# Decode attention on one core: values seven heads behind the keys, another choice of groups whose value product streams V, and two heads' output rows multiplied earlier

## Chip, cores, metric

One core of one Trainium2 chip. The metric is the device time of one execution in microseconds (us); the profile's span is 1.7 to 1.9 us shorter, as it leaves out the ends (2.0 to 3.0 us in three runs of before_64). PE is the matmul engine, PEld its weight loads, DVE, ACT and POOL the vector, scalar and general engines, SP the engine that issues the loads.

## The reference

A decode step for one token. The part that fills the time is attention over 32 heads, each with 4096 keys and values of 128 elements in bf16: 1 MB of keys and 1 MB of values per head.

```python
q = (x @ wq).reshape(B, Sq, Hq, Dh)...            # 32 heads of 128
k = k_cache[:, :, Sk - W:, :]; v = v_cache[...]     # W = 4096
p = softmax(einsum("bhqd,bhkd->bhqk", q, k) * Dh**-0.5)
o = einsum("bhqk,bhkd->bhqd", p, v)
s = o.reshape(B, Sq, Hq * Dh) @ wo                  # wo: 4096 x 512
# ... x + s * g, where g comes from a small MLP
```

## The kernel before

The kernel is one software pipeline over the heads. In step `i` it loads and handles the keys of head `i`, and the values of head `h = i - LAG`. Even heads get their scores on DVE (`k_vector`), odd heads on PE (`k_turn`, `k_scores`). Four heads form a group that shares a softmax.

The value product (PV) has two forms. In the ordinary one V is the stationary operand and 32 matmuls of one column make `o`; in the "moved" one V streams through PE, in 8 matmuls of 512 columns:

```python
MOVED = (1, 4); LAG = 6; K_BUFS = 12; V_BUFS = 7
...
def v_head(h, v):
    if g in MOVED:
        for c in range(0, NC, 4):
            nc.tensor.matmul(s["ov"][32 * hl:32 * hl + 4], lhsT=s["pT"][:, hl, c:c + 4],
                             rhs=v[:, c:c + 4, :], ...)
    else:
        for c in range(NC):
            nc.tensor.matmul(s["oT"][:, hl:hl + 1], lhsT=v[:, c, :], rhs=s["pT"][:, hl, c:c + 1], ...)
```

The tail, where the change works (cuts are marked `...`):

```python
for i in range(H + LAG):
    h = i - LAG
    kn = load_kv(k_pool, A_k_cache, i) if i < H else None
    ...
    if h == H - 1:
        load_rows(h_part, H - G - h_part)      # wo rows of heads 26, 27
    v = load_kv(v_pool, A_v_cache, h) if h >= 0 else None
    ...
    if h == H - 1:
        load_rows(H - G, G - 1)                # heads 28 to 30
        load_rows(H - 1, 1)                    # head 31: the last load
    ...
    if i == H:
        v_head(h, v); sm_turn(LG); y_block(few_block - 1); sm_exp(LG); ox_spread(few_block)
    ...
    if h >= H - G:
        v_out(h, 1)                            # ACT: o of head h, divided by its sum

for h in range(h_part, H):                     # 6 heads, 24 matmuls
    y_head(h)                                  # o of head h times its rows of wo
```

## Time and profile before

| | before |
|---|---|
| time, median of the first 3 runs | 197.33 us (197.11 to 197.45) |
| span of the profiled run | 196.0 us |
| loads from HBM | 78.84 MB, 402 GB/s over the span |
| busy: PE, DVE, ACT | 71%, 64%, 43% |
| chain that ended last, by engine | DMA 69%, PE 21%, issue 4% |

The row of DMA in the page's slices tells that transfers fill the time from the start to the last two slices. The chain of waits tells what the very end hangs on. It is found from the end backwards and printed in order of time: each piece is what released the next one. Both are shown in the prediction.

### The profile page before, as it was taken

The numbers are of one execution on the slowest core, as the hardware profiler recorded it, in microseconds if no ns is written. First come the engines' busy times: TensorE is split into PE (matmuls) and PEld (weight loads), VectorE is DVE, ScalarE is ACT, GpSimd is POOL, SyncE is SP. The second block draws the span as 40 slices with busy tenths as digits, with TensorE's granted clock in tenths as the row PEclk, the third lists the DMA queues.
The fourth block names the chain that finished last, engine by engine and source line by source line (L and its number), as shares of the span: only waits on it lengthen the run. The fifth ranks groups of instructions, "written<-read, shape, count | busy, mean of one in ns | idle before, by whom it ended". The sixth has DMA issues, their size and how long they took to land.

```text
span 196.0 us, 4913 instructions
## 1 busy us (share of the span) xinstructions
PE 138.4 (71%) x2204; PEld 105.6 (54%) x2204; DVE 124.7 (64%) x124; ACT 84.5 (43%) x180; POOL 5.9 (3%) x13
## 2 busy tenths in 40 slices
PE   0559797672796899787785828399977757289752
PEld 0453435561795555486365817335547756178542
DVE  1520259998988949795969195495979391853001
ACT  2003028870757443946074707407282619064210
POOL 2110007000000000000000000000000000000000
PEclk9999859967555579995596555759997558558555
DMA  6999899999999999999999999999999999999970
GB/s 199 408 476 448 363 413 420 418 428 428 423 428 420 428 418 428 418 428 423 428 421 428 421 428 425 423 428 423 426 426 421 426 421 428 423 426 426 414 270 4
DMA packets 11516, 79.15 MB, mean 404 GB/s; under 512 B 1384, under 2 KB 2248, under 8 KB 2504
## 3 DMA queue, kind: packets, MB, share of 16 engines
q1 hardware_dynamic: 11344, 78.85, 96.3%
q8 instruction: 17, 0.28, 0.6%
q10 hardware_dynamic: 152, 0.00, 0.0%
q14 instruction: 3, 0.02, 0.0%
HBM read 78.84 MB, written 0.00 MB: 402 GB/s over the span
## 4 chain that ended last, share of the span: by engine, by line
DMA 69%; PE 21%; issue 4%; DVE 2%; ACT 1%; POOL 1%; SPq 0%; POOLq 0%
DMA kv<-in_A_v_cache_dram 37%; DMA kv<-in_A_k_cache_dram 30%; PE oT L389 3%; PE qb_ps L240 3%; PE ov L379 3%; PE pt L290 3%; DMA x_bf<-in_A_x_dram 2%; PE hr_ps L214 2%; PE y_ps L141 1%; PE a_ps L203 1%; PE hr_ps L211 1%; PE qT_ps L231 1%; PE sT L297 1%; PE den_ps L334 1%; ACT kt L291 1%
## 5 line engine op out<-in xcount | busy, mean ns | idle before, releaser
L291 ACT COPY kt<-pt 128x1024 bf16<-128x1024 bf16 x64 | 60.2, 1028 | 58.9 <-PE pt L290 58.9
L281 DVE TENSOR_REDUCE sS<-prod 128x32 f32<-128x4096 bf16 x16 | 70.7, 4420 | 0.6
L290 PE MATMUL pt<-ident_bf,kv 128*128 128x128 bf16 x512 | 46.0, 268 | 8.4 <-DMA kv<-in_A_k_cache_dram 6.9
L290 PEld LDWEIGHTS <-kv 128*128 128x128 bf16 x512 | 41.9, 124 | 13.2 <-DMA kv<-in_A_k_cache_dram 7.9
L278 DVE TENSOR_TENSOR prod<-kv,q_bc 128x4096 bf16<-128x4096 bf16 x16 | 36.6, 2288 | 14.1 <-DMA kv<-in_A_k_cache_dram 11.8
L389 PE MATMUL oT<-pT,kv 128*128 128x1 bf16 x768 | 23.8, 165 | 15.3 <-DMA kv<-in_A_v_cache_dram 10.8
L389 PEld LDWEIGHTS <-kv 128*128 128x128 bf16 x768 | 22.9, 103 | 17.2 <-DMA kv<-in_A_v_cache_dram 12.0
L379 PE MATMUL ov<-kv,pT 128*4 128x512 bf16 x64 | 18.5, 441 | 0.0
L297 PE MATMUL sT<-qT_bf,kt 128*128 128x1 bf16 x512 | 16.3, 164 | 2.5 <-ACT kt L291 2.3
L297 PEld LDWEIGHTS <-kt 128*128 128x128 bf16 x512 | 14.7, 99 | 4.8 <-ACT kt L291 3.0
L404 ACT ACTIVATE o<-oT,rden 128x1 bf16<-128x1 f32 x32 | 6.1, 263 | 13.9 <-PE oT L389 9.3
L336 DVE RECIPROCAL rden<-den_ps 128x4 f32<-128x4 f32 x8 | 1.5, 182 | 14.7 <-PE den_ps L334 14.7
L379 PEld LDWEIGHTS <-pT 128*4 128x4 bf16 x64 | 5.3, 92 | 10.2 <-issue 5.4
L311 PE MATMUL mt_ps<-ident_f,m 128*4 128x128 f32 x8 | 2.5, 315 | 6.4 <-DVE m L305 5.9
L321 PE MATMUL mb_ps<-md,ones_f 4*128 4x4 f32 x16 | 3.6, 292 | 4.4 <-DVE md L315 4.4
L313 DVE TENSOR_REDUCE mx<-mt_ps 4x1 f32<-4x128 f32 x8 | 2.2, 278 | 7.0 <-PE mt_ps L311 7.0
L321 PEld LDWEIGHTS mb_ps<-md,ones_f 4*128 4x128 f32 x16 | 2.9, 223 | 6.5 <-DVE md L315 6.5
L240 PE MATMUL qb_ps<-wq_sb,xn_rep 128*128 128x512 bf16 x16 | 6.3, 584 | 0.0
L217 DVE COPY hr<-hr_ps 1x512 f32<-1x512 f32 x1 | 0.7, 679 | 8.4 <-PE hr_ps L214 8.4
L443 PE MATMUL yr_ps<-wo,ox 128*1 128x512 bf16 x16 | 5.2, 483 | 0.0
L323 ACT COPY mb<-mb_ps 128x4 f32<-128x4 f32 x8 | 1.5, 185 | 8.6 <-PE mb_ps L321 8.6
L206 ACT ACTIVATE a_bf<-a_ps 128x10 bf16<-128x10 f32 x1 | 0.2, 179 | 11.5 <-PE a_ps L203 11.5
(110 smaller groups left out, 94.1 us busy)
## 6 DMA issues: line engine op xcount, KB each, us to landing
kv<-in_A_k_cache_dram SPq DMA_DIRECT2D x32, 1024.0 KB, 19.6
kv<-in_A_v_cache_dram SPq DMA_DIRECT2D x32, 1024.0 KB, 19.6
wq_sb<-in_A_wq_dram SPq DMA_DIRECT2D x1, 4096.0 KB, 18.1
wo<-in_A_wo_dram SPq DMA_DIRECT2D x3, 1024.0 KB, 20.3
w_sb<-in_B_w_dram SPq DMA_DIRECT2D x1, 1376.0 KB
w_sb<-in_B_w_dram SPq DMA_DIRECT2D x1, 1024.0 KB, 8.9
w_sb<-in_B_w_dram SPq DMA_DIRECT2D x1, 512.0 KB, 3.7
wo_rows<-in_A_wo_dram SPq DMA_DIRECT2D x1, 384.0 KB, 16.3
```

The lines of the kernel that those rows point to most:

```text
L214: nc.tensor.matmul(hr_ps[:], lhsT=a_bf[0:m, i:i + 1], rhs=w4_sb[0:m, i, :], start=False, stop=(i == len(chunks) - 1))
L240: nc.tensor.matmul(qb_ps[:], lhsT=xn_rep[:, c, :], rhs=wq_h[:, c, 2 * i:2 * i + 8:2, :], start=(c == 0), stop=(c == KC - 1))
L278: nc.vector.tensor_tensor(out=prod[:], in0=kn[:], in1=q_bc[:, h // 2:h // 2 + 1, :].to_broadcast([P, NC, Dh]), op=ALU.mult)
L281: nc.vector.tensor_reduce(out=st[g]["sS"][:, hl // 2, :], in_=prod[:], axis=AX.X, op=ALU.add)
L290: nc.tensor.transpose(pt[:, i, :], kn[:, b * 8 + i, :], ident_bf[:])
L291: nc.scalar.copy(out=kts[h][:, b * 8:(b + 1) * 8, :], in_=pt[:])
L297: nc.tensor.matmul(st[g]["sT"][:, hl // 2, c:c + 1], lhsT=kt[:, c, :], rhs=qT_bf[:, h:h + 1], start=True, stop=True)
L321: nc.tensor.matmul(mb_ps[:], lhsT=ones_f[0:G, :], rhs=s["md"][:], start=True, stop=True)
L379: nc.tensor.matmul(s["ov"][32 * hl:32 * hl + 4], lhsT=s["pT"][:, hl, c:c + 4], rhs=v[:, c:c + 4, :], start=False, stop=c == NC - 4, skip_g ...
L389: nc.tensor.matmul(s["oT"][:, hl:hl + 1], lhsT=v[:, c, :], rhs=s["pT"][:, hl, c:c + 1], start=(c == 0), stop=(c == NC - 1))
L404: nc.scalar.mul(o_blk[h // 8][:, (h + k) % 8:(h + k) % 8 + 1], st[g]["oT"][:, hl + k:hl + k + 1], st[g]["rden"][:, hl + k:hl + k + 1])
L443: nc.tensor.matmul(yr[i][:], lhsT=ox_blk[i][:, t:t + 1], rhs=wo_blk[i][:, t, :], start=(t == 0), stop=(t == 7))
```

## The change

The intent is to give PE one more step between a group's softmax and its value products, so that PE is not behind the loads at the end, and to take work out of the last stretch. The core of the diff:

```diff
-LAG = 6
+LAG = 7
-MOVED = (1, 4)
+MOVED = (2, 4)
...
-        if h == H - 1:
+        if h == H - 2:
             load_rows(h_part, H - G - h_part)
...
-            for g in done(i, LAG + 5):
+            for g in done(i, LAG + 4):        # ox_spread, ox_pick; y_wide moves likewise
...
-            for g in done(i, LAG + 1, LG):
+            for g in done(i, G + 3, LG):
                 sm_den(g)
...
         if h >= H - G:
             v_out(h, 1)
+        if h == H - 2:
+            for r in range(h_part, H - G):    # heads 26 and 27, right after PV30
+                y_head(r)
-    for h in range(h_part, H):
+    for h in range(H - G, H):
         y_head(h)
```

The rest of the diff sorts the last seven steps anew.

More of the change, by code (lines that the diff above doesn't have):

```diff
@@ L503 @@
                 sm_exp(g)
-            for g in done(i, LAG + 1, LG):
+            for g in done(i, G + 3, LG):
                 sm_den(g)
-            for g in done(i, LAG + 5):
+            for g in done(i, LAG + 4):
                 if g % 2 == 1:
@@ L509 @@
         if i == H:
-            v_head(h, v)
             sm_turn(LG)
@@ L514 @@
             sm_exp(LG)
-            ox_spread(few_block)
-        elif h >= 0:
-            if i == H + 1:
-                ox_pick(few_block)
-            if i == H + 2:
-                ox_few(few_block)
-                sm_den(LG)
-            v_head(h, v)
-            if i == H + 2:
-                y_block(few_block)
+        if i == H + 1:
+            ox_pick(few_block)
+        if i == H + 2:
+            ox_few(few_block)
+            sm_den(LG)
+        if h >= 0:
+            v_head(h, v)
+        if i == H:
+            v_out(H - 2 * G, 2)
+            ox_spread(few_block)
+        if i == H + 2:
+            y_block(few_block)
+            rows_add(y_ps, one_f, y_row, False)
+        if i == H + 3:
+            v_out(H - 2 * G + 2, 2)
         if i < H:
@@ L532 @@
                     v_out(G * g, G)
-            for g in done(i, LAG + 6):
+            for g in done(i, LAG + 5):
                 if g % 2 == 1:
@@ L536 @@
                     y_keep(g // 2)
-        if i == H - 1:
-            v_out(H - 2 * G, 2)
-        if i == H + 1:
-            v_out(H - 2 * G + 2, 2)
-            rows_add(y_ps, one_f, y_row, False)
         if h >= H - G:
             v_out(h, 1)
-    for h in range(h_part, H):
+        if h == H - 2:
+            for r in range(h_part, H - G):
+                y_head(r)
+    for h in range(H - G, H):
         y_head(h)
```

## The prediction

> **What bounds the kernel now.** I read the page first: the totals and the slices, then the DMA view, then the chain that ended last, and last the timeline of the final 25 us. The slices come first, because an average would hide what differs by stage.
>
> ```profile
> PE   0559797672796899787785828399977757289752
> PEclk9999859967555579995596555759997558558555
> DMA  6999899999999999999999999999999999999970
> GB/s 199 408 476 448 363 413 420 418 428 428 423 428 420 428 418 428 418 428 423 428 421 428 421 428 425 423 428 423 426 426 421 426 421 428 423 426 426 414 270 4
> ...
> q1 hardware_dynamic: 11344, 78.85, 96.3%
> q8 instruction: 17, 0.28, 0.6%
> ```
>
> The DMA row has a 9 in every slice from the sixth to the thirty-eighth, at some 425 GB/s. No engine has that: PE is at 71% of the span, DVE at 64%, ACT at 43%. So the kernel is a stream of 78.85 MB that must pass (78.85 MB at 425 GB/s is 185.5 us of the 196.0), a start before the stream is full, and a tail after the last bytes. The change loads the same tensors in the same pieces, so it cannot shorten the stream. It can only touch what the end waits for. That is in the chain:
>
> ```profile
> 180.74 0.83 PE oT L389 x32
> 181.57 0.53 PE y_ps L141 x6
> 182.10 1.04 issue
> 183.13 0.58 PE y_ps L141 x2
> ...
> 186.56 0.96 PE oT L389 x32
> ...
> 187.86 0.83 PE oT L389 x26
> 188.69 1.40 issue
> 190.10 0.31 PE oT L389 x6
> ...
> 190.43 0.27 ACT o L404
> ...
> 190.75 0.99 PE oT L389 x32
> 191.74 0.77 PE y_ps L141 x13
> ```
>
> The groups of 32 are the value products (PV) of heads 27, 29, 30 and 31 (28 is in between). Two things are to be seen. From 172 us on, the chain is on PE and no longer on a DMA, so PE is behind the stream. And two pauses called "issue" (1.04 and 1.40 us) break it in the middle of instructions that wait for no data. How far behind PE is follows from the landing times of the last loads:
>
> ```profile
> 172.27 0.34 SPq L77 DMA_DIRECT2D kv<-in_A_v_cache_dram  x1
> DMA to landing us min/median/max: 17.7/17.7/17.7
> ...
> 177.06 2.32 SPq L77 DMA_DIRECT2D wo_rows<-in_A_wo_dram  x1
> ```
>
> The first two lines are the load of V31, the values of the last head: it lands at 172.27 + 17.7 = 189.97 us, and its product starts at 190.75, so PE is 0.78 us late. The third is the last load of all, the output rows of head 31. By the DMA view of its own window it takes 14.2 us to landing: 177.06 + 14.2 = 191.26 us. The last four matmuls, which need those rows, end at 191.74 + 0.77 = 192.51 us. So PE's lateness is worth little: about 1 us lies between the last landing and the end of PE.
>
> **What the skill says.** "DMA: Bandwidth & Descriptors", section "Where 436 GB/s comes from", puts the ceiling of 16 engines at 435 GB/s. The trace agrees with 425 to 428 in the plateau: there is nothing left in it. "Runtime: NRT & Kernel Launch", section "Instruction fetch mechanics", says that an engine's instructions come by DMA in blocks of 16 KiB, that is 256 instructions, mostly hidden. The trace has 17 packets with 0.28 MB on the instruction queue, 16 KB each, and I take the two pauses for fetches that were not hidden, as PE runs a dense stretch there: from the first pause to the second it runs about 256 instructions. "TensorE: Matmul & The Clock Gate", Part 1, says that the array runs at half or full clock by its recent activity. The trace agrees: 32 PV matmuls take 0.78 us where the granted clock was 0.93 (176 to 180 us) and 0.99 us at 0.50 in the tail. I expect the tail at 0.50 after the change too.
>
> **The change part by part.**
>
> Values seven heads behind the keys. K7 goes into the queue ahead of V0, and every later key is one load ahead of where it was against the values. A 1 MB load takes 2.45 us (the keys and values are issued at that distance: 62.17, 64.68, 67.11). K31 landed at 172.21 with seven values still to come, and should land at about 169.8 with eight to come. K30, for DVE, moves by more than that, since the third block of output weights now stands between K30 and K31. The softmax of the last group and the scores of head 31, which made PE late, thus move about 2.45 us earlier, while V31 stays at 189.97. That more than covers the lateness of 0.78 us. At the start the queue holds one more load when V0 has to wait for the end of the weights' use (V0 is issued at 30.52; the queue waited 9.0 us for the query product). The queue did not run dry there before (413 and 420 GB/s in the slices around it), so nothing is gained.
>
> Rows of heads 26 and 27 at PV30. They are 8 matmuls out of the 24 that ran after PV31. Rows of 24 took 192.51 - 191.74 = 0.77 us after PV31, so 8 of them are worth at most 0.77 x 8/24 = 0.26 us. But the rows of head 31 also wait for ACT's o of head 31, about 0.3 us after PV31 ends (0.27 us and two waits of 0.02 to 0.04), during which the first rows run for nothing. Of the 0.26 about 0.2 should be seen. Their load moves ahead of V30 and delays V30 by some 0.6 us (256 KB), to 187.5, which is not what the end waits for.
>
> V through PE for groups 2 and 4 in place of 1 and 4. The matmul is moved, not added: 64 of 379 to 441 ns and two of 0.6 us before and after. It is some 3 us dearer per head than the 0.8 to 1.0 us of the other form, 12 us in a group, in a stretch where the stream has 19.6 us per four heads. PE was busy for 9.50 us of 70 to 80 and 9.52 of 130 to 140, and recovered within a few slices. I expect no change of the time from it: the queue is eight loads deep, 19.6 us from issue to landing, and waited for PE only 1.2 us in total.
>
> The instruction fetch. The instruction count on PE is the same but for two, so the block ends in the same place counted from the end: about the 25th matmul of PV30. From the two fetches I estimate that a block is asked for half a block (128 instructions) ahead and comes almost 4 us later. PV28 to PV30 will be further apart in time, since they wait for their loads, so the second pause should shrink from 1.40 to some 0.2 to 1.1 us and end before V31 lands or just with it.
>
> Sum: PV31 starts at 190.0 to 190.2 in place of 190.75 (0.55 to 0.75 us gained). It ends 0.99 later, at 191.0 to 191.2, ACT's o is there 0.3 later, at 191.3 to 191.5, just after the last rows have landed (191.26), and the last four matmuls add 0.4 to 0.45: PE ends at 191.7 to 191.95 in place of 192.51. The gain is 0.55 to 0.8 us; I take 0.7. The two DVE operations and the store of the output behind it stay (192.53 to 196.0). 197.3 - 0.7 = 196.6 us.
>
> **The rivals.**
>
> The last landing bounds all of it, and moves. The end cannot come before 191.26 + 0.4. The sixteen DMA engines do not end together: the DMA view of 184 to 192 us falls from some 400 GB/s to some 250 and then to 50 before it stops, so one late engine sets the last landing. If the new order makes it later by 1 us, the gain is gone: 197.3 to 197.6. If it is earlier by 1 us, PE follows it as far as V31 allows: 195.6. Against both speaks that bytes, pieces and engines are the same.
>
> The fetch pause stays whole. If it falls at the same place of PV30 with 1.40 us, PV31 starts at 190.7 as before, and only the moved rows are gained: 197.1 us. For it speaks that V30 arrives at 187.5, where PV30 also begins now (187.86).
>
> PE falls behind in the middle. With groups 2 and 4 there is one ordinary group between the dear ones where there were two. If PE were late by more than the eight loads of the queue can take, keys' buffers would come free late, the stream would have a hole, and the time would grow by its length, 1 to 4 us. Against it: in the table of stretches PE is busy for 5.49 us of 110 to 120 and 5.97 of 120 to 130, so what one dear group leaves behind is worked off before the next.
>
> A lasting gain in the stream by the deeper lead. It would need holes to fill; the slices show none after the sixth. I give it little.
>
> **Range and chances.** Predicted 196.6 us. The low end is the landing a microsecond earlier with no pause, 195.5. The high end is the landing 0.3 us later with a whole pause, 197.5. Two per cent is 3.95 us: faster than 193.4 would need an end of PE at 188.6, before V31 has landed, so 0.02. Slower than 201.3 needs a hole in the stream of 4 us: 0.02. Within 2%: 0.96.
>
> **What would show each step.** Right: the slices again at 425 GB/s; K31's transposes begin at about 169.8; the chain of the last 10 us holds a wait for V31 and PV31 starts within 0.3 us of its landing; 16 rows, not 24, after PV31; the last pause called "issue" shorter than 1.1 us; PE ends at 191.7 to 192.0. Wrong: a V31 or a last row that lands more than 0.5 us from 189.97 and 191.26 (then the stream, not PE, made the difference), a pause of 1.4 us inside PV30 or PV31, or a slice under 400 GB/s between 30 and 180 us.

## The result

| | before | changed |
|---|---|---|
| first measurement, 6 runs each, median | 197.28 us | 196.91 us (196.49 to 197.72) |
| ratio | | 0.9983, 95% interval 0.9961 to 1.0005 |
| repeated (first experiment below), 11 and 6 runs | 197.29 us | 196.70 us (196.43 to 198.09) |
| ratio | | 0.9976, interval 0.9942 to 1.0010 |

A ratio is the mean time of one kernel's fast runs over that of the other's of the same rounds, so it is not quite the ratio of the medians. Both intervals contain 1.000: the times alone show neither a gain nor a loss. What changed inside is much clearer in the profile.

Profile after, the DMA row, the rate and the instruction queue of the page:

```profile
DMA  5999999999999999999999999999999999999980
GB/s 193 408 467 430 384 421 425 413 423 430 421 425 420 423 426 425 421 421 428 430 425 421 421 430 430 423 425 420 428 428 423 425 421 426 423 428 427 421 327 12
...
q8 instruction: 17, 0.28, 0.6%
```

The stream is the same: the same plateau of some 425 GB/s, the same 17 instruction packets. Its last load, the rows of head 31, is issued at 177.14 and takes 14.2 us to landing: 191.34 us, where it was 191.26.

The end of the chain of waits (start us, length us, what):

```profile
169.89 3.59 PE pt L290 x32
...
175.16 14.84 DMA kv<-in_A_v_cache_dram
189.99 0.04 issue
190.04 1.01 PE oT L389 x32
191.05 0.66 PE y_ps L141 x15
```

The chain now goes straight from the landing of V31 (175.16 + 14.84 = 190.00) to its product. Before, it ran on PE from 172 us to the end. K31's transposes start at 169.89 in place of 172.25. PV31 starts 0.04 us after its values land, where it was 0.83 us late. (The trace holds sixteen semaphore increments for a load, taken here as one for the share of each of the sixteen DMA engines. By the last of them V31 landed at 189.92 us in the kernel before; the prediction's 189.97 adds a landing time that was rounded to 17.7.) PE ends at 191.05 + 0.66 = 191.71 in place of 192.51.

The timeline of PE in the last stretch after the change (start us, busy us, engine, line, operation, tiles, count, and in brackets the idle time before and what ended it):

```profile
187.64 1.10 PE L389 MATMUL oT<-pT,kv 128*128 128x1 bf16 x32 [0.69 <-DMA kv<-in_A_v_cache_dram]
188.68 0.38 PE L141 MATMUL y_ps<-wo_rows,o 128*1 128x128 bf16 x8
...
190.04 1.01 PE L389 MATMUL oT<-pT,kv 128*128 128x1 bf16 x32 [0.98 <-DMA kv<-in_A_v_cache_dram]
191.05 0.63 PE L141 MATMUL y_ps<-wo_rows,o 128*1 128x128 bf16 x16
```

PV30 is one piece of 1.10 us; before it was 26 matmuls, a pause of 1.40 us and 6 more. PE waits for data ahead of both products, so it is no longer late. The 8 row matmuls run in the wait for V31. The other 16 run behind PV31; their last four wait for `o` of head 31, as the weight loads of the same timeline show:

```profile
191.40 0.09 PEld L141 LDWEIGHTS <-o 128*1 128x1 bf16 x4 [0.16 <-ACT o L404]
```

So PE ends 0.80 us earlier in these two profiles, while the medians differ by 0.37 and 0.59 us. The profiled run of before took 197.79 us, half a microsecond above its median, and the stream itself varies by as much: over the profiles of kernels with 17 instruction packets and all loads, V31 lands between 189.3 and 190.0 us in all but one. So from here on PE's end is taken against the landing of V31 in the same profile. The lateness of the kernel before comes from one profile; two near copies of it, rows_only and moved_only below, have 0.60 and 0.67 us.

### The profile page after: what moved, and what is told of

Same layout as the page of the kernel before. It is cut to its first block, busy times and chain, and to the rows that moved or that the text cites. A ratio compares the mean times of both kernels' runs of the same rounds, so it can differ in the third digit from the quotient of the medians.

```text
span 195.2 us, 4912 instructions
## 1 busy us (share of the span) xinstructions
PE 134.2 (69%) x2204; PEld 107.8 (55%) x2204; DVE 124.6 (64%) x124; ACT 85.0 (44%) x180; POOL 5.9 (3%) x13
## 4 chain that ended last, share of the span: by engine, by line
DMA 81%; PE 12%; issue 3%; DVE 2%; ACT 1%; POOL 1%; SPq 1%; POOLq 0%
DMA kv<-in_A_k_cache_dram 51%; DMA kv<-in_A_v_cache_dram 28%; PE pt L290 2%; DMA x_bf<-in_A_x_dram 2%; PE qb_ps L240 2%; PE hr_ps L214 2%; PE a_ps L203 1%; PE hr_ps L211 1%; PE oT L389 1%; PE qT_ps L231 1%; SPq L77 1%; ACT kt L291 1%; DVE hr L217 0%; PE y_ps L141 0%; PE ln_ps L158 0%
## 5 line engine op out<-in xcount | busy, mean ns | idle before, releaser
L290 PE MATMUL pt<-ident_bf,kv 128*128 128x128 bf16 x512 | 48.6, 277 | 18.6 <-DMA kv<-in_A_k_cache_dram 17.1
L290 PEld LDWEIGHTS <-kv 128*128 128x128 bf16 x512 | 44.3, 129 | 22.5 <-DMA kv<-in_A_k_cache_dram 19.6
L389 PEld LDWEIGHTS <-kv 128*128 128x128 bf16 x768 | 22.9, 104 | 12.3 <-DMA kv<-in_A_v_cache_dram 9.7
L379 PE MATMUL ov<-kv,pT 128*4 128x512 bf16 x64 | 15.7, 389 | 1.0 <-DMA kv<-in_A_v_cache_dram 1.0
L321 PEld LDWEIGHTS mb_ps<-md,ones_f 4*128 4x128 f32 x16 | 3.6, 275 | 6.7 <-DVE md L315 6.5
L321 PE MATMUL mb_ps<-md,ones_f 4*128 4x4 f32 x16 | 4.3, 334 | 4.4 <-DVE md L315 4.4
L311 PEld LDWEIGHTS mt_ps<-ident_f,m 128*4 128x4 f32 x8 | 0.7, 94 | 10.1 <-issue 6.2
```

The lines of the kernel that those rows point to most:

```text
L290: nc.tensor.transpose(pt[:, i, :], kn[:, b * 8 + i, :], ident_bf[:])
L311: nc.tensor.transpose(mt_ps[:], s["m1"][:], ident_f[:])
L321: nc.tensor.matmul(mb_ps[:], lhsT=ones_f[0:G, :], rhs=s["md"][:], start=True, stop=True)
```

## The experiments

Eleven builds ran, on two chips, each beside the kernel before on its own chip: the first four below on one, the others on another, where the changed kernel itself did not run. This is how all that load V31 compare. The landing of V31 is its issue plus its length in the chain; where the chain does not hold that load (before, rows_only, moved_only) it is the last of its sixteen semaphore increments. The end of PE is the end of the last piece of `y_ps` in the chain.

| run | time, median us | ratio, 95% interval | V31 lands | PV31 starts after | PE ends after |
|---|---|---|---|---|---|
| before (its one profile) | 197.28 | | 189.92 | 0.83 | 2.59 |
| changed | 196.91 | 0.9983 (0.9961 to 1.0005) | 190.00 | 0.04 | 1.71 |
| again | 196.70 | 0.9976 (0.9942 to 1.0010) | 189.32 | 0.05 | 1.72 |
| lag_only | 196.75 | 0.9980 (0.9945 to 1.0015) | 189.52 | 0.04 | 1.83 |
| rows_only | 196.87 | 0.9974 (0.9946 to 1.0002) | 189.34 | 0.60 | 2.25 |
| moved_only | 198.00 | 1.0031 (0.9990 to 1.0071) | 189.68 | 0.67 | 2.43 |
| before_64 | 198.64 | 1.0055 (1.0022 to 1.0089) | 192.03 | 0.05 | 1.84 |
| after_97 | 197.69 | 1.0023 (0.9988 to 1.0058) | 190.65 | 0.05 | 1.72 |
| blocks4 | 197.95 | 1.0023 (0.9983 to 1.0063) | 190.99 | 0.05 | 1.72 |
| drop_rows | 196.71 | 0.9969 (0.9932 to 1.0006) | 189.76 | 0.05 | 1.71 |
| moved3 | 196.51 | 0.9966 (0.9932 to 1.0000) | 189.76 | 0.05 | 1.73 |
| v8 (one look, state unknown) | 196.53 | | 189.53 | 0.06 | 1.73 |

### again: the changed kernel once more

No edit.

> The changed kernel as it is, to narrow the first interval (0.9961 to 1.0005). Theory (PE's lateness of 0.78 us is gone, the last landing bounds the end): 0.3 to 0.8 us under the kernel before, ratio 0.996 to 0.9985; PV31 starts within 0.1 us of the landing of V31. Rival (no real change, the first profile was a lucky one): ratio 1.000, and the place of PV31 wanders from run to run.

The ratio is within what was expected, and the interval is no help: runs of the kernel before went from 196.50 to 198.92 us on this chip. The place of PV31 does not wander: 0.05 us after the landing, as in the first profile. The rival of a lucky profile falls; that the time is lower is not shown. One of the prediction's own signs of being wrong came here: V31 landed at 189.32 and the last row at 190.69, each 0.6 us earlier than in the kernel before. So of PE's end in this profile, 191.04, some 0.6 us is the stream's and not PE's.

### lag_only: without the moved rows

```diff
-        if h == H - 2:
+        if h == H - 1:
             load_rows(h_part, H - G - h_part)
...
-        if h == H - 2:
-            for r in range(h_part, H - G):
-                y_head(r)
-    for h in range(H - G, H):
+    for h in range(h_part, H):
```

> Values seven heads behind and groups 2 and 4, but the 8 row matmuls of heads 26 and 27 stay at the end and their load stays just ahead of V31. Theory: PV31 starts at 190.0 to 190.1 as in the changed kernel, 24 row matmuls follow it, the end is 0.2 us later than in the changed kernel (PE ends at 191.9). Rival (the moved rows are what helps): the whole gain is gone, PE ends at 192.5.

The chain of waits of this run ends so:

```profile
189.56 1.01 PE oT L389 x32
190.58 0.77 PE y_ps L141 x14
```

PV31 follows its values at once, without the moved rows, and the row matmuls take 0.77 us as in the kernel before. Of the 2.59 - 1.71 = 0.88 us that PE won against the landing, the lag (with its groups and the new order of the last steps) brings 2.59 - 1.83 = 0.76. These three were not tested apart. PE ends 0.11 to 0.12 us later than in the changed kernel, where 0.2 was expected. PV30 still holds a pause of 0.73 us here, after its 27th matmul, and ends at 188.36, over a microsecond before V31 lands: the pause is there and costs nothing.

### rows_only: the moved rows in the kernel before

```diff
-        if h == H - 1:
+        if h == H - 2:
             load_rows(h_part, H - G - h_part)
...
+        if h == H - 2:
+            for r in range(h_part, H - G):
+                y_head(r)
-    for h in range(h_part, H):
+    for h in range(H - G, H):
```

> The kernel before with the 8 row matmuls and their load moved ahead, all else as before (values six heads behind). Theory: PE stays late and the pause inside PV30 stays, PV31 starts at about 190.75 as before, and only the rows are gained: PE ends 0.2 us earlier than 192.51. Rival (rows are the gain): PE ends at 191.7 to 191.9.

The chain of waits of this run, before the last rows:

```profile
187.05 0.83 PE oT L389 x26
187.88 1.40 issue
189.28 0.30 PE oT L389 x6
189.58 0.31 PE y_ps L141 x4
189.89 0.04 issue
189.94 0.99 PE oT L389 x32
```

The pause stays in the same place and with the same length, and PV31 is 0.60 us late. PE ends 2.59 - 2.25 = 0.34 us earlier against the landing; 0.2 was expected. Only 0.11 us of it lies behind PV31, where the row matmuls take 0.66 us in place of 0.77. The other 0.23 is an earlier start of PV31, and what of that the rows brought is not shown: between the end of PV30 and PV31 they save nothing (0.36 us, 0.34 before), while the first pause was shorter in this profile, 0.19 in place of 1.04 us. In absolute time PE ends at 191.59, even below the 191.7 to 191.9 of the rival; V31 landed 0.58 us earlier in this profile than in that of before, which is the stream's doing. The times cannot tell the parts apart: 196.75, 196.87 and 196.70 us for the lag, the rows and both.

### moved_only: groups 2 and 4 in the kernel before

```diff
-MOVED = (1, 4)
+MOVED = (2, 4)
```

> The kernel before with groups 2 and 4 through PE in place of 1 and 4, nothing else. Theory: no change of the time (ratio 0.999 to 1.001), the last landing as before at 191.3; the pauses of PE stay at the same instructions. Rival (this part shifts PE work away from the end): PV31 starts earlier than 190.6.

In the profile the tail is that of the kernel before: PV30 is cut after its 26th matmul, by 1.68 us, and PV31 is 0.67 us late. So the other choice of groups does not remove the lateness by itself. The rival's sign, a start before 190.6, did come (190.35), but V31 landed 0.24 us earlier too, so only 0.16 us of it is PE's. The time came out 0.31% above the kernel before, outside the expected 0.1%, with an interval that contains 1.000. Its six runs go from 196.73 to 198.93 us and those of before on that chip from 196.50 to 198.92. Whether this part alone costs something stays open.

### before_64: needless matmuls that move the pauses

```diff
         for g in done(i, G):
             sm_max(g)
+        if i == G:
+            scrap = ps_misc.tile([P, 1], FP32, tag="misc", name="scrap")
+            for _ in range(64):
+                nc.tensor.matmul(scrap[:], lhsT=zero_bf[:], rhs=ident_bf[:, 0:1], start=True, stop=True)
```

> The kernel before with 64 needless matmuls (128 instructions with their weight loads) added on PE at about 43 us, where PE stands idle for some 4 us; nothing else. Theory (the pauses called issue are instruction fetches that come every 256 instructions): both pauses move 128 instructions earlier, so the one inside PV30 is gone, PV31 starts within 0.3 us of the landing of V31 in place of 0.7 to 0.8, and the kernel gets 0.3 to 0.7 us faster though it does more. Rival (the pause belongs to PV30, a wait for data that the trace does not show): the pause stays after the 26th matmul of PV30 and the time is the same.

The timeline of PE at the end of this run:

```profile
187.85 1.01 PE L389 MATMUL oT<-pT,kv 128*128 128x1 bf16 x32 [1.01 <-DMA kv<-in_A_v_cache_dram]
192.08 1.02 PE L389 MATMUL oT<-pT,kv 128*128 128x1 bf16 x32 [3.22 <-DMA kv<-in_A_v_cache_dram]
193.03 0.81 PE L141 MATMUL y_ps<-wo_rows,o 128*1 128x128 bf16 x24
```

About PE the theory held. PV30 runs without a pause and PV31 follows its values in 0.05 us, in the kernel before with nothing but 128 instructions more. That PV31 is on time would not prove it alone, as V31 landed 2.1 us later and K31 only 1.0 us later than in the kernel before. But from the landing of K31 to the end of PV30 PE took 188.86 - 173.20 = 15.66 us, a wait of 1.01 us for V30 included, in place of 190.41 - 172.21 = 18.20: the two pauses (2.44 us) are gone. Those matmuls do no work that the tail needs, so the pauses go by the instruction count, as block fetches do.

Two readings of the kept traces settle it. In all thirteen profiles, PE stands still for over 0.5 us after 40 us, with nothing in the trace that it waits for, in seven places. Counted in the instructions that the trace records for PE, five of them come after exactly 4289 (before, rows_only, moved_only, lag_only, and blocks4 below, where that is another head's product, at 157 us) and two after 4033 (before, moved_only): 256 apart. And each ends 2.3 to 2.5 us after a packet of the instruction queue has begun: in the kernel before packets begin at 180.7 and 187.7, and the pauses end at 183.13 and 190.10.

About the time the theory failed: the kernel is 0.55% slower, not faster, since V31 lands at 192.03, some 2 us later. Of that 1.2 us is a slow start of this one profile, the slowest of the six runs: the query weights land at 22.43 us in place of 21.27, long before the needless matmuls. The rest called for a new question: do the needless instructions delay the loads? (Part of the longer time lies outside the profiled span: the medians differ by 1.43 us, those of the spans by 0.75.)

### after_97: the block border in PV31

The same edit on the changed kernel with 97 in place of 64.

> The changed kernel with 97 needless matmuls (194 instructions) at the same place. Theory of the fetches: the block border moves from the 25th matmul of PV30 to the middle of PV31; the fetch is asked for 128 instructions ahead, when PE is at PV30, and comes almost 4 us later, so PV31 is cut by a pause of 0.7 to 1.7 us, PE ends 0.7 to 1.5 us later than in the changed kernel against the landing of V31, and the kernel is no better than the one before, or worse. Rival: PV31 runs in 1.0 us as in the changed kernel and the time is the same.

No pause came. PE stood waiting for V30 for 2.56 us ahead of PV30 in this run, and the fetch fell into that wait (the DMA view of 185 to 188.4 us has one instruction packet). PV31 ran in 1.01 us. My estimate of when a block is asked for and when it comes was too coarse to place a pause inside a tail that waits for data. The kernel seems slower all the same, by 0.8 to 1.0 us against the changed kernel's medians on the other measurements (against the kernel before on its own chip its interval contains 1.000), and the lateness is again in the stream: the profile has 18 instruction packets in place of 17 and V31 lands at 190.65.

That gave a second theory. The trace has the sixteen increments of most loads, one per DMA engine. For the last load, in the kernel before, the first engine's share lands at 187.34, four are in by 188.2, the other twelve land from 189.8 to 191.26. So the engines end far apart, and the last one sets the landing. In both runs with needless matmuls one share stands 1.0 us behind the rest of the late ones; in the changed kernel's two profiles the last share is 0.0 to 0.4 us behind its neighbour. A block of 16 KB may hold up the one engine that fetches it; the packets of the instruction queue take 0.92 to 1.13 us each.

The early loads of the kernel before, where the blocks come one at a time, show it:

| load, by its last landing | blocks fetched by then, at | shares behind the others | by |
|---|---|---|---|
| 21.27 us | none | 0 of 16 | |
| 27.67 us | 25.1 | 1 | 1.4 us |
| 40.07 us | 25.1, 36.5 | 2 | 1.4 us |
| 54.79 us | 25.1, 36.5, 51.9 | 3 | 1.4 us |

The late shares stay late from load to load. In before_64, with its needless matmuls, the third block comes at 42.8, and there the load that lands at 48.69 has three late shares already; in the kernel before the load that lands at 47.43 has two.

### blocks4: four more blocks

```diff
+        if 4 <= i < H - 2:
+            scrap = ps_misc.tile([P, 1], FP32, tag="misc", name="scrap")
+            for _ in range(20):
+                nc.tensor.matmul(scrap[:], lhsT=zero_bf[:], rhs=ident_bf[:, 0:1], start=True, stop=True)
```

> The changed kernel with 520 needless matmuls (1040 instructions, four more blocks of 16 KB), 20 in each of 26 steps, where PE has idle time. Theory formed from the last two runs (each fetched block holds up one of the sixteen DMA engines by about 1 us, so more blocks make the last landing later): 21 or 22 packets on the instruction queue in place of 17, the first engine's share of the last load lands as before at 187.3 to 187.5, the last engine's at 192 to 193 in place of 190.7 to 191.3, and the time rises by 0.7 to 1.5 us. Rival (the later landings of the last two runs were chance): last landing 190.7 to 191.4, time within 0.3 us of the changed kernel.

The instruction queue of this run's page, and the end of its chain of waits:

```profile
q8 instruction: 21, 0.34, 0.7%
```

```profile
175.52 15.47 DMA kv<-in_A_v_cache_dram
191.00 0.05 issue
191.04 1.01 PE oT L389 x32
192.05 0.66 PE y_ps L141 x16
```

Every number came as expected: 21 packets, the first engine's share of the last load at 187.46, the last one's at 192.29, four shares 0.9 us or more behind the other twelve, and 197.95 us, which is 1.0 to 1.25 us over the changed kernel's medians. On its own chip, too, all four of its runs (197.74 to 198.01) lie above the ten of drop_rows and moved3 (196.18 to 197.53), where PE ends as early behind V31 (1.71 and 1.73 us). PE is not late: its piece behind V31 is the 1.72 us of the changed kernel, and loads issued later would have delayed the first engine's share too. So the delay sits in single DMA engines. It does not simply grow with the number of blocks. From the first share of the last load to its last one it is 3.92 us in the kernel before and 4.77 in before_64, both with 17 packets, 4.77 in after_97 with 18, 4.83 here with 21, and 3.80 in moved3 with 16. The engine that lost most sets the landing, and which engine takes a block is not told by the trace.

### drop_rows: without the last two loads (wrong)

```diff
         if h == H - 1:
-            load_rows(H - G, G - 1)
-            load_rows(H - 1, 1)
+            pass
...
-        return wo_rows[:, h - h_part, :]
+        return wo_rows[:, (h - h_part) % 2, :]
```

> Wrong on purpose: the last two loads (512 KB, the rows of heads 28 to 31) are left out and the rows of heads 26 and 27 are used in their place. The last landing is then V31. If the last landing as such bounds the end (rival), PE ends 1.2 us earlier. If the chain behind V31 does (its product 1.0 us, o 0.3, the last matmuls 0.35), PE ends as before, 1.7 us after the landing of V31, and the time falls by less than 0.2 us.

The end of the chain of waits:

```profile
174.91 14.85 DMA kv<-in_A_v_cache_dram
189.76 0.05 issue
189.81 1.01 PE oT L389 x32
190.82 0.66 PE y_ps L141 x9
```

Without the last 512 KB PE ends 1.71 us after V31, as with them. So it is V31 and the chain behind it that the end waits for, and the last rows, which land 1.34 us after V31 in the changed kernel, are just early enough. The time, 196.71 us, is that of the changed kernel on the other chip.

### drop_v31: without the last values (wrong)

```diff
-        v = load_kv(v_pool, A_v_cache, h) if h >= 0 else None
+        if h < H - 1:
+            v = load_kv(v_pool, A_v_cache, h) if h >= 0 else None
```

> Wrong on purpose: V31 is not loaded and PV31 uses the values of head 30. The stream is 1 MB, 2.45 us, shorter. If the stream sets the end wholly, the time falls by 2.4 us. If PE's chain behind V30 takes over (V30 lands at 187.6, PV30 1.0, o 0.3, PV31 1.0, o 0.3, rows 0.35), PE ends at 190.5 and the time falls by 1.2 us. If PE were still late as in the kernel before, it falls by less than 0.5 us.

The end of the chain of waits:

```profile
170.89 17.67 DMA kv<-in_A_v_cache_dram
188.56 0.05 issue
188.61 1.02 PE oT L389 x32
...
189.98 0.99 PE oT L389 x32
190.97 0.66 PE y_ps L141 x9
```

The median is 196.20 us over four runs, 195.21 to 196.83: a ratio of 0.9933 (0.9891 to 0.9976) to the kernel before. Against the changed kernel, from which the edit starts, the medians fall by 0.5 to 0.7 us, and by 0.5 against drop_rows on the same chip; the expected 1.2 us shows only between the lowest runs of the two. So the time alone does not tell the second branch of the expectation from the third. The profile does: PE waits for V30 and is not late, and behind V30 the chain took 3.07 us (191.63 - 188.56), against 2.9 in the expectation. The stream became shorter by 2.45 us and the kernel by much less, as PE's own chain of two products takes over. The profile fell on one of the two longer runs (V30 landed at 188.56), so the expected end of PE at 190.5 was not met.

### moved3: one more group through PE

```diff
-MOVED = (2, 4)
+MOVED = (0, 2, 4)
```

> The changed kernel with group 0 through PE as well: 96 matmuls of PE fewer by 189 instructions, about 12 us more PE time early, where PE has idle time. Theory of the blocks: 16 packets in place of 17 or the same 17, last landing 0 to 0.5 us earlier, time 0 to 0.5 us under the changed kernel; a candidate for a better version. Rival (PE's extra time costs more): time above the changed kernel, with PE's idle time before its transposes gone.

As expected, 16 instruction packets in place of 17; the last load lands at 191.07, within the spread of the changed kernel's two profiles (191.34 and 190.69). The time is 0.9966 of the kernel before, which cannot be told from the changed kernel's 0.9976. It is a candidate, not a better version that was shown.

### v8: a value buffer more, a key buffer fewer

```diff
-K_BUFS = 12
+K_BUFS = 11
-V_BUFS = 7
+V_BUFS = 8
```

> The changed kernel with eight buffers for values and eleven for keys. In the changed kernel the load of V31 was issued 2.8 us late, as it waits for PV24 to free its buffer. Theory: that wait is hidden by the loads that are queued ahead, so with it gone V31 is issued at about 172.4 in place of 175.2 and lands at the same time, within 0.4 us of 190.0 (taken against the last landing). Rival: V31 lands 1 us or more earlier.

The first piece of its chain's end:

```profile
171.84 17.69 DMA kv<-in_A_v_cache_dram
```

V31 is issued 3.3 us earlier than in the changed kernel (175.16) and lands at 189.53 against 190.00 and 189.32 in that kernel's two profiles. The wait of the load for a free buffer is hidden behind the loads queued ahead, as expected.

## Why the prediction was right or wrong

**The stream stays.** Right. 425 GB/s as before, and the last landing at 191.34 against 191.26. The deeper lead of the keys brought nothing to it. Run to run it moves: in `again` the last landing is 190.69.

**K31 2.45 us earlier.** Right: 172.25 to 169.89, 2.36 us.

**PV31 at 190.0 to 190.2.** Right: 190.04, and lag_only shows that the lag with its groups does it alone.

**The moved rows, about 0.2 us.** Right in kind, and half the size. Behind PV31 they save 0.77 - 0.66 = 0.11 us, both on top of the lag (1.83 - 1.72) and alone (rows_only). The term that was mis-sized is ACT's `o` of head 31: with 24 matmuls nothing waits for it, with 16 the last four do, by 0.16 us (0.23 in rows_only), so that of the 0.26 us some 0.15 are hidden, not 0.06.

**The pause.** The reason held: the pauses go by the instruction count (before_64). The size was off: 0.2 to 1.1 us was expected to remain inside PV30, and in the changed kernel's two profiles 0.1 us and nothing did (1.10 and 1.01 us in all). In lag_only it was 0.73 us and in v8 0.37. The part of the forecast that mattered, that the pause ends before V31 lands, held in all of them. The step that failed is the estimate of when a block is asked for and comes, "half a block ahead" and "almost 4 us later". When a block is asked for the trace does not tell; from the start of its packet to the end of the pause it shows 2.3 to 2.5 us. after_97 failed by the same estimate.

**Groups 2 and 4.** "No change of the time" is neither shown nor refuted: moved_only was 0.31% slower with an interval of -0.10% to +0.71%. The price was too high, if without effect: 8 matmuls of 379 ns (the median; 441 is the mean) take 3.0 to 3.5 us, 2 to 2.7 us more per head than the other form, and not 3. What I had not seen is that the choice was not free.

**A buffer wait that I had not named.** V31 is issued 2.8 us later than its turn, as it waits for PV24. It is the new wait that the deeper lag brought, and v8 shows it hidden.

**The sum.** PE ends at 191.71, the early end of 191.7 to 191.95, and 196.91 us (later 196.70) stands against 196.6. The gain in medians, 0.37 and 0.59 us, is smaller than 0.7. The 0.8 us that PE won is a difference between two profiles, that of before was one of its longer runs, and the spread of the stream from run to run is as large; what of the difference each makes is not shown. The time within the range says little: 195.5 to 197.5 also holds the 197.3 of the kernel before. What bears the prediction out is the place of PV31, in both profiles and in lag_only.

**The clock.** The clock granted to PE in the tail stayed at 0.50 of full speed, as expected. But 0.78 and 0.99 us for 32 products do not show what the clock does: the 0.78 is a piece of the chain, cut where the product overlaps the work before it. In the timeline the same products take 0.94 us at a clock of 0.93 and 0.99 to 1.01 at 0.50. Only the 0.99 of the tail went into the sum.

**The rival of the last landing.** I gave it as a shift by luck. It is in part a real term: the landing depends on which engines fetch the instruction blocks, about 1 us for blocks4 and its four. The change keeps the count at 17 and the distance from first to last share at 3.9 and 3.3 us (3.92 before), so no part of it is seen there; that the count alone does not settle it, before_64 shows.

## What to carry to other kernels

Where the loads fill the time, ask how late the last consumer is against the landing of the last load: that lateness is most of what a new order of the tail can win (here 0.79 of 0.88 us; the rest is work taken out of the chain behind the landing), and it is best measured in the profile against the landing, as the landing itself moves from run to run. Look for pauses in a dense tail that belong to no data; they can be instruction fetches, and a tail that waits for its loads hides them. Instructions of an engine are not free in a kernel bound by its loads, as their blocks come over the same DMA engines: here 520 needless matmuls, on an engine with idle time, cost about a microsecond.

## What the Trainium skill lacked or had wrong

- "Runtime: NRT & Kernel Launch", section "Instruction fetch mechanics", calls the fetch of a block mostly hidden. In the dense tail of the kernel before it was not: PE paused 1.04 and 1.40 us, and 128 needless instructions moved the pause out of PV30 (before_64). Wherever such a pause of over 0.5 us shows, it comes after the same count of PE's recorded instructions, 4033 or 4289, 256 apart.
- The same section does not say that fetched blocks delay the loads. Each of the first three blocks of the kernel before put one more of the sixteen engines 1.4 us behind. With 21 blocks in place of 17 the last load landed at 192.29 in place of 190.69 to 191.34, and the median time was 1.0 to 1.25 us longer (blocks4).
- "DMA: Bandwidth & Descriptors", section "Why a DMA increments its semaphore by 16 and not by 1", says that the engines finish independently. The trace agrees; the page gives no size. Here the shares of one 128 KB load land over 3.9 us (187.34 to 191.26), which is more than the 2.45 us of a whole 1 MB load in the plateau.
